# Dropping the zero columns behind the last K and Q heads and keeping one column of ones per chunk of three heads

## The chip, the cores and the metric

The kernel runs on one core of one Trainium2 chip. The core has a matrix engine (TensorE, PE in the profile; its weight loads are listed as PEld), a vector engine (VectorE, DVE), an activation engine (ScalarE, ACT), a general engine (GpSimd, POOL) and a queue that issues the DMAs (SyncE, SP). They run side by side and wait for each other through semaphores. The metric is the time of one execution on the device in microseconds (us); the time of a kernel is the median of its runs.

## The reference: what is computed

The input is 2048 tokens of 640 channels in bfloat16. They are normalized (layer norm without weights), and two branches are added to the input:

```python
xn  = layernorm(x)
out = x + A(xn) + B(xn)

# A: linear attention, H = 32 heads of Dh = 20 channels
q, k, v = split_heads(xn @ wqkv)
pq, pk  = q @ w_phi, k @ w_phi                       # per head, 20 x 20
phi_q   = concat(softmax(pq), softmax(-pq))          # 40 features per head
phi_k   = concat(softmax(pk), softmax(-pk))
kv      = phi_k^T v          # per head, summed over all tokens: 40 x 20
z       = sum of phi_k over the tokens               # 40
A       = ((phi_q kv) / (phi_q z + 1e-6)) @ wo

# B: gated linear unit with F = 1536
B       = (silu(xn @ w1) * (xn @ w3)) @ w2
```

## The kernel before, in words

Tokens are worked on in 16 tiles of 128 (`NST`), channels in 5 chunks of 128 (`KD`). Everything is written inside a manual schedule: each engine does its instructions in the order in which the code issues them, and the code interleaves the stages by hand.

The 32 heads are grouped in 11 chunks (`NCH`): ten of three heads and a last one of two (`HC`). A chunk takes 2 x 64 features: 60 of the positive softmax (three heads of 20), 4 of padding, and the same for the negative one, so that the features of one chunk fill 128 rows of the matrix engine. The last chunk has only 40 real features of each sign. The kernel keeps its shape by computing a 33rd head of zeros: the fused weights `wkphi` and `wqphi` have `FW` = 660 columns for 640 real ones, and the last 20 columns, filled with zeros by GpSimd in the first channel chunk (L190), are multiplied for that chunk alone (L300). Their exponentials are 1, so nothing special has to be done behind them. In a loop on the chip that runs only where the weights are too large for an exponential without its maximum taken off, the same helpers are used; it does not run here.

The stages, in order of time:

- *Start.* Inputs are loaded, layer norm statistics go through VectorE and GpSimd, xn is transposed (on TensorE and ScalarE for the first four tiles, by DMA for the others). `v_unit` (L311) computes V of a tile: ten matmuls of 320 columns in two PSUM banks, which ScalarE copies to `vaug` (L314) in two pieces. `vaug` holds, for each tile and each head, 20 channels of V and one 1, so that one matmul yields kv and z; the ones are filled once, by ScalarE for half the tiles (L196) and by GpSimd for the others (L200). GLU units (`glu_unit`, L398: ten matmuls of 512 columns; ScalarE takes a tanh, VectorE two products) are put between. Late in this stage `fuse` (L382) multiplies the key weights with `w_phi`; ScalarE copies the results to `wkphi` (L391), in turn with the copies of the last V units, in the order V(12), FB(0), FB(1), V(13), FB(2), V(14), FB(3), V(15), FB(4).
- *K rounds*, 16 of them. `phi_unit` multiplies a tile by `wkphi` (ten matmuls, L301, 360 columns in one bank and 280 or 300 in the other), ScalarE takes four exponentials (`exps`, L328: two signs for each of two banks), VectorE sums them by head (L361) and takes reciprocals (L363), GpSimd scales (L364). Two rounds later `kv_unit` (L424) multiplies phi, as weights, by the chunk's rows of `vaug` (63 columns, 42 for the last chunk) and adds up in a pair of PSUM banks kept through all rounds. GLU units fill the round; in five rounds `fuse` makes the query weights.
- *Q rounds*, 20 of them. The same for queries; in the second one `kv_done` (L437) copies the sums of `kv_unit` to `kvr`, leaving out with a mask (`own`) the products of one head's features with another's channels: three products on VectorE. phi is transposed by a DMA (L444), `r_unit` (L453) multiplies it by `kvr`, VectorE divides (L469 to L474), the result is transposed by a DMA (L499), and from the fifth round on `out_unit` (L516) multiplies by `w2` and `wo` and VectorE adds the input (L525).

Single PSUM banks come from one pool of six (`bank`), shared by V, fused weights, K, Q, GLU and output units; one double bank (`pair`) serves `kv_unit`, `r_unit` and every other `fuse`.

Of the kernel before, what the change touches and what calls it, by code (L numbers as in the profile page):

```python
# [8 lines left out]
P = 128  # L9
# [3 lines left out]
def kernel(  # L13
# [36 lines left out]
    NCH = 11  # L50
    HC = [3] * 10 + [2]
    CH = 6 * 3 * Dh

    FW = D + Dh

    PARTS = [
        (0, 0, 0, 7), (0, 1, 6, 13), (0, 2, 12, 16),
# [6 lines left out]
    one = ctx.enter_context(tc.tile_pool(name="one", bufs=1))  # L64
    work = ctx.enter_context(tc.tile_pool(name="work", bufs=2))
# [3 lines left out]
    def bank(name, dt=f32):  # L69
        n = 512 if dt == f32 else 1024  # L70
        return psum.tile([P, n], dt, name=name, tag="bank")

    def pair(name):
        return psum2.tile([P, 2, 512], f32, name=name, tag="pair")


    xnT = one.tile([P, KD, S], bf, name="xnT")
    wkphi = one.tile([P, KD, FW], bf, name="wkphi")
    wqphi = one.tile([P, KD, FW], bf, name="wqphi")
    w1 = one.tile([P, KD, F], bf, name="w1")  # L80
# [15 lines left out]
    wkT, wqT, wv = w_nat[:, 0], w_nat[:, 1], w_nat[:, 2]  # L96
# [1 line left out]
    phiqT = reg_w[:, KD * D : KD * D + 4 * NCH * P].rearrange(  # L98
        "p (n c s) -> p n c s", n=4, c=NCH
    )  # L100
    vaug = reg_v[:].rearrange("p (t h e) -> p t h e", t=NST, e=21)
    w2 = reg_v[:, 0 : KF * D].rearrange("p (c d) -> p c d", c=KF)
    oT = reg_v[:, KF * D : KF * D + KD * 512].rearrange("p (c s) -> p c s", c=KD)
    less = phi[:, 1].rearrange("p c g f -> p (c g f)")[:, 0 : 2 * FW].bitcast(f32)
# [14 lines left out]
    with tc.manual_schedule():  # L119
# [14 lines left out]
        def ld_wv(c, n):  # L134
# [21 lines left out]
            out=mask[:], in_=mask[:], pattern=[[8, KD], [-20, 8]], base=0,  # L156
# [3 lines left out]
            out=mask[:], in_=mask[:], pattern=[[-8, KD], [20, 8]], base=19,  # L160
# [4 lines left out]
        own = one.tile([P, 2, 3], bf, name="own")  # L165
        nc.gpsimd.memset(own[:], 1.0)
        nc.gpsimd.affine_select(
            out=own[:], in_=own[:], pattern=[[-64, 2], [-20, 3]], base=0,
# [3 lines left out]
            out=own[:], in_=own[:], pattern=[[64, 2], [20, 3]], base=19,  # L172
# [6 lines left out]
        nought = one.tile([P, P], bf, name="nought")  # L179
# [6 lines left out]
        warm(WARM)  # L186

        nc.gpsimd.memset(phi[:, :, :, :, 60:64], 0.0)
        for w in (wkphi, wqphi):
            nc.gpsimd.memset(w[:, 0, D:FW], 0.0)  # L190

        table = one.tile([P, 1], f32, name="table")
        nc.scalar.activation(out=table[:], in_=nought[:, 0:1], func=AF.Sqrt)
        nc.scalar.activation(  # L196
            out=vaug[:, 0:8, :, 20].rearrange("p t h -> p (t h)"),
            in_=nought[:, 0:1].to_broadcast([P, 8 * H]), func=AF.Identity, bias=1.0,
        )
        nc.gpsimd.memset(vaug[:, 8:NST, :, 20], 1.0)  # L200


        mv = one.tile([P, NST, 2], f32, name="mv")
# [85 lines left out]
        def tile_of(t):  # L289
            return slice(t * P, (t + 1) * P)  # L290

        def by_token(cols, w, name, cut, between=(KD, None)):


            ps = [bank(name), bank(name)]
            for c in range(KD):
                if c == between[0]:
                    between[1]()
                for i in range(2):
                    a, b = (0, cut) if i == 0 else (cut, w.shape[2] if c == 0 else D)  # L300
                    nc.tensor.matmul(  # L301
                        ps[i][:, 0 : b - a],
                        xnT[:, c, cols],
                        w[:, c, a:b],
                        start=(c == 0),
                        stop=(c == KD - 1),
                        skip_group_check=True,
                    )
            return ps

        def v_unit(t, cols=None, between=(KD, None)):  # L311
            ps = by_token(cols or tile_of(t), wv, "pv", HD, between)
            for i in range(2):
                nc.scalar.copy(  # L314
                    out=vaug[:, t, 16 * i : 16 * i + 16, 0:20],
                    in_=ps[i][:, 0:HD].rearrange("p (h d) -> p h d", d=Dh),
                )

        def halves(ps, dst):

            for i, n in ((0, 6), (1, 5)):
                c = slice(6 * i, 6 * i + n)
                yield ps[i][:, 0 : 60 * n], [dst[:, c, g, 0:60] for g in range(2)], n

        def exps(ps, dst):
            for p, to, n in halves(ps, dst):
                for g in range(2):
                    nc.scalar.activation(  # L328
                        out=to[g], in_=p.rearrange("p (c f) -> p c f", f=60),
                        func=AF.Exp, scale=1.0 - 2.0 * g,  # L330
                    )

        def exps_less_max(ps, dst):

            h0 = 0
            for p, _, n in halves(ps, dst):
                nc.scalar.copy(out=wide[:, Dh * h0 : Dh * (h0 + 3 * n)], in_=p)
                h0 += 3 * n
            w3 = wide[:, 0:FW].rearrange("p (h d) -> p h d", d=Dh)
            for g, op in ((0, ALU.max), (1, ALU.min)):  # L340
                top = work.tile([P, FW // Dh], f32, name="top")
                nc.vector.tensor_reduce(out=top[:], in_=w3, axis=AX.X, op=op)
                nc.gpsimd.tensor_tensor(
                    out=less[:].rearrange("p (h d) -> p h d", d=Dh), in0=w3,
                    in1=top[:, :, None].to_broadcast([P, FW // Dh, Dh]), op=ALU.subtract,
                )
                nc.scalar.activation(
                    out=dst[:, :, g, 0:60], in_=less[:].rearrange("p (c f) -> p c f", f=60),
                    func=AF.Exp, scale=1.0 - 2.0 * g,
                )  # L350

        def phi_unit(t, w, name, exps=exps, cols=None):

# [66 lines left out]
        def kv_unit(t, acc, first, last):  # L420

            for c in range(NCH):
                b, i = divmod(c, 6)
                nc.tensor.matmul(  # L424
                    acc[:, b, 63 * i : 63 * i + 21 * HC[c]],
                    phi[:, t % 4, c].rearrange("p g f -> p (g f)"),
                    vaug[:, t, 3 * c : 3 * c + HC[c], :],
                    start=(first and i == 0),
                    stop=last,
                    skip_group_check=True,  # L430
                )

        def kv_done(acc):

            for b, c0, n, k in ((0, 0, 6, 3), (1, 6, 4, 3), (1, 10, 1, 2)):
                a = 63 * (c0 - 6 * b)
                nc.vector.tensor_mul(  # L437
                    out=kvr[:, c0 : c0 + n, 0:k, :],
                    in0=acc[:, b, a : a + 21 * k * n].rearrange("p (c i e) -> p c i e", c=n, e=21),
                    in1=own[:, 0:1, 0:k, None].to_broadcast([P, n, k, 21]),  # L440
                )

        def phi_transposed(t):
# [250 lines left out]
        acc = pair("pkv")  # L694
# [51 lines left out]

    ok = nc.values_load(flag[0:1, 0:1], min_val=0, max_val=1)
    with tc.If(ok == 0):
        state = reg_v[:, 2048 : 2048 + 4 * 378].bitcast(f32).rearrange("p (b e) -> p b e", b=2)
        ld(wv, w_of(2))  # L750
        nc.gpsimd.memset(vaug[:, 0, :, 20], 1.0)
        nc.gpsimd.memset(state, 0.0)
        with tc.For_i(0, NST, 1) as t:
            cols = bass.ds(t * P, P)
            v_unit(0, cols)
            phi_unit(0, wkphi, "pk", exps_less_max, cols)
            acc = pair("pkv")
            kv_unit(0, acc, True, True)
            for i, n in ((0, 378), (1, 315 - 21)):
                nc.vector.tensor_tensor(  # L760
                    out=state[:, i, 0:n], in0=state[:, i, 0:n], in1=acc[:, i, 0:n], op=ALU.add
                )
        kv_done(state)
        ld(w2, B_w2.rearrange("(c p) d -> p c d", p=P))
        with tc.For_i(0, NST, 1) as t:
            rows = bass.ds(t * P, P)
            phi_unit(0, wqphi, "pq", exps_less_max, rows)
            phi_transposed(0)
            r_unit(0, quotient_by_pool)
            o_transposed(0)  # L770
            h = hT[:, bass.ds(t, 1)].rearrange("p a f s -> p (a f) s")
            res = out_unit(h, slice(0, P), residual(rows))
            ld(out2[rows, :], res[:])
# [28 lines left out]
```

## Time and profile before

| | |
|---|---|
| median of 3 runs | 271.1 us (270.97 to 271.72) |
| the profiled execution, its own time | 272.32 us |
| its span in the profile | 270.5 us |
| TensorE busy | 264.7 us, 98% of the span |
| VectorE, ScalarE, GpSimd busy | 188.5, 110.1 and 95.7 us |
| granted TensorE clock | full in all 40 slices |

The profile is of one execution; its rows are in microseconds from the start of the span. A group row names the line, the engine, the operation, the tiles written and read with their shapes, the count, then the busy time and the mean length of one in nanoseconds, and behind the next bar the idle time of the engine ahead of it and what ended it. A row of the chain has a start, a length, an engine and a line; the chain is followed back from the last instruction through whatever released each. A row of the timeline has a start, a length, an engine, an instruction and, in brackets, the idle time ahead.

### The profile page before, as it was taken

To read this page: it belongs to the slowest core of one execution; us is meant where nothing else is said; L and a number is where in the kernel's file an instruction comes from. 1 tells how busy PE (TensorE), PEld (TensorE's weight loads), DVE (VectorE), ACT (ScalarE), POOL (GpSimd) and SP (SyncE) were. 2 spreads that over 40 slices of the span, in tenths; PEclk is the share of its full clock that TensorE was granted. 3 is DMA by queue.
4 is the path that set the end of the run, shared out by engine and by line. 5 is a ranking of instruction groups with operands and counts; after the bars stand their busy time and mean duration, and the time that the engine had idled before them with its cause. 6 is when DMAs were issued, how large, how long until landed. Compare 5 with 4: busy or idle time off the path is not lost.

```text
span 270.5 us, 5193 instructions
## 1 busy us (share of the span) xinstructions
PE 264.7 (98%) x1990; PEld 166.6 (62%) x1990; DVE 188.5 (70%) x345; ACT 110.1 (41%) x263; POOL 95.7 (35%) x100
## 2 busy tenths in 40 slices
PE   8899999999999999999999999999999999999995
PEld 8546567555555555555555445677777777777773
DVE  4699950787777667777777788876766777776341
ACT  5653468543555554435655545422222222221000
POOL 5054740344443333333444321333344444433000
PEclk9999999999999999999999999999999999999999
DMA  6996547980000000000000864356676755675931
GB/s 200 339 242 121 68 87 181 299 197 28 0 0 2 0 2 0 0 5 0 0 2 0 221 179 84 82 121 137 117 151 137 142 129 126 130 148 129 152 98 55
DMA packets 63100, 27.80 MB, mean 103 GB/s; under 512 B 50144, under 2 KB 61792, under 8 KB 63072
## 3 DMA queue, kind: packets, MB, share of 16 engines
q1 hardware_dynamic: 63072, 27.43, 45.2%
q8 instruction: 17, 0.28, 0.4%
q14 instruction: 11, 0.09, 0.1%
HBM read 12.81 MB, written 2.62 MB: 57 GB/s over the span
## 4 chain that ended last, share of the span: by engine, by line
PE 89%; DVE 4%; DMA 2%; POOL 2%; issue 1%; SPq 1%; ACT 0%; DVEq 0%
PE acc L516 27%; PE gp L398 18%; PE up L398 18%; PE pq L301 8%; PE pk L301 8%; PE pv L301 5%; DMA reg_w<-in_A_wqkv_dram 2%; PE pkv L424 2%; PE pr L453 2%; DVE st L210 1%; PE pf L382 1%; SPq L109 1%; DVE reg_h L264 1%; POOL ry L224 1%; DVE gs L411 0%
## 5 line engine op out<-in xcount | busy, mean ns | idle before, releaser
L364 POOL TENSOR_TENSOR phi<-phi,rk 128x1320 bf16<-128x1320 bf16 x32 | 77.2, 2413 | 134.5 <-DVE rk L363 134.5
L361 DVE TENSOR_REDUCE sk<-phi 128x66 f32<-128x1320 bf16 x32 | 48.9, 1528 | 41.4 <-ACT phi L328 40.4
L398 PEld LDWEIGHTS <-w 128*128 128x128 bf16 x480 | 45.6, 98 | 50.6
L301 PEld LDWEIGHTS <-xnT 128*128 128x128 bf16 x480 | 45.3, 97 | 23.3 <-issue 2.0
L398 PE MATMUL up<-xnT,w 128*128 128x512 bf16 x240 | 59.6, 379 | 0.0
L398 PE MATMUL gp<-xnT,w 128*128 128x512 bf16 x240 | 59.6, 378 | 0.0
L516 PE MATMUL acc<-reg_v,reg_h 128*128 128x320 bf16 (+2 forms) x384 | 54.9, 299 | 0.0
L328 ACT ACTIVATE phi<-pq 128x360 bf16<-128x360 f32 (+1 forms) x64 | 23.3, 450 | 59.2 <-POOL phi L364 53.8
L516 PEld LDWEIGHTS <-reg_h 128*128 128x128 bf16 x384 | 37.3, 98 | 14.4
L406 ACT ACTIVATE th<-gp 128x512 f32<-128x512 f32 x48 | 28.8, 600 | 34.0 <-PE gp L398 30.4
L414 DVE SCALAR_TENSOR_TENSOR reg_h<-gs,up 128x512 bf16<-128x512 bf16 x48 | 33.0, 688 | 4.9
L328 ACT ACTIVATE phi<-pk 128x360 bf16<-128x360 f32 (+1 forms) x64 | 23.3, 451 | 24.5 <-PE pk L301 15.5
L411 DVE SCALAR_TENSOR_TENSOR gs<-th,gp 128x512 bf16<-128x512 f32 x48 | 31.5, 657 | 0.3 <-ACT th L406 0.3
L525 DVE TENSOR_TENSOR res<-acc,xr 128x320 bf16<-128x320 f32 (+2 forms) x32 | 14.3, 487 | 21.5 <-PE acc L516 21.5
L301 PE MATMUL pv<-reg_w,xnT 128*128 128x320 bf16 x160 | 23.9, 299 | 1.4 <-DMA reg_w<-in_A_wqkv_dram 1.1
L301 PE MATMUL pk<-wkphi,xnT 128*128 128x360 bf16 (+2 forms) x160 | 24.7, 300 | 0.0
L301 PE MATMUL pq<-wqphi,xnT 128*128 128x360 bf16 (+2 forms) x160 | 24.6, 299 | 0.0
L516 PE MATMUL acc<-reg_w,reg_v 128*128 128x320 bf16 (+2 forms) x160 | 24.5, 299 | 0.0
L363 DVE RECIPROCAL rk<-sk 128x66 f32<-128x66 f32 x32 | 18.1, 567 | 3.2
L516 PEld LDWEIGHTS <-reg_v 128*128 128x128 bf16 x160 | 15.7, 98 | 6.1
L210 DVE BATCH_NORM_STATS2 st<-reg_h 128x6 f32<-128x320 bf16 x32 | 13.8, 470 | 3.9 <-DMA reg_h<-in_A_x_dram 3.9
L314 ACT CAST reg_v<-pv 128x320 bf16<-128x320 f32 x32 | 12.1, 433 | 8.3 <-PE pv L301 8.2
(67 smaller groups left out, 134.6 us busy)
## 6 DMA issues: line engine op xcount, KB each, us to landing
w<-in_B_w_dram SPq DMA_DIRECT2D x2, 1280.0 KB, 8.8
xr<-in_A_x_dram SPq DMA_DIRECT2D x16, 160.0 KB, 2.5
out_dram<-res SPq DMA_DIRECT2D x15, 160.0 KB, 1.8
reg_h<-in_A_x_dram SPq DMA_DIRECT2D x7, 320.0 KB, 5.5
reg_v<-in_B_w_dram SPq DMA_DIRECT2D x4, 480.0 KB, 5.2
w<-in_B_w_dram SPq DMA_DIRECT2D x4, 320.0 KB, 6.6
reg_w<-in_A_wqkv_dram SPq DMA_DIRECT2D x2, 320.0 KB, 5.4
reg_w<-in_A_wo_dram SPq DMA_DIRECT2D x1, 480.0 KB, 4.3
```

Source lines behind the costliest of these rows:

```text
L210: nc.vector.bn_stats(out=st[:, i, :], in_=xt[:, i * HD : (i + 1) * HD])
L301: nc.tensor.matmul(ps[i][:, 0 : b - a], xnT[:, c, cols], w[:, c, a:b], start=(c == 0), stop=(c == KD - 1), skip_group_check=True,)
L328: nc.scalar.activation(out=to[g], in_=p.rearrange("p (c f) -> p c f", f=60), func=AF.Exp, scale=1.0 - 2.0 * g,)
L361: nc.vector.reduce_sum(out=sk[:], in_=rows, axis=AX.X)
L363: nc.vector.reciprocal(out=rk[:], in_=sk[:])
L364: nc.gpsimd.tensor_mul(out=rows, in0=rows, in1=rk[:, :, :, None].to_broadcast([P, 2 * NCH, 3, Dh]))
L398: nc.tensor.matmul(ps[:], w[:, c, fi * P : (fi + 1) * P], xnT[:, c, sc * 512 : (sc + 1) * 512], start=(c == 0), stop=(c == KD - 1),)
L406: nc.scalar.activation(out=th[:], in_=gp[:], func=AF.Tanh, scale=0.5)
L411: nc.vector.scalar_tensor_tensor(out=gs[:], in0=th[:], scalar=1.0, in1=gp[:], op0=ALU.add, op1=ALU.mult)
L414: nc.vector.scalar_tensor_tensor(out=hT[:, 4 * sc : 4 * sc + 4, fi, :], in0=gs[:].rearrange("p (t s) -> p t s", t=4), scalar=0.5, in1=up[: ...
L516: nc.tensor.matmul(ps[:, 0 : b - a], rows[j][0], rows[j][1][:, a:b], start=(j == 0), stop=(j == len(rows) - 1),)
L525: nc.vector.tensor_tensor(out=res[:, a:b], in0=ps[:, 0 : b - a], in1=xr[:, a:b], op=ALU.add)
```

## The change

The zero columns go. `wkphi` and `wqphi` get 640 columns, their GpSimd fills go, and the second bank of a K or Q unit gets 280 columns in every channel chunk. The 20 features of each sign that the last chunk has too many are filled once with ones in all four phi buffers, by GpSimd; they are summed and scaled with the others as before.

`vaug` holds one column of ones for each chunk of three heads, at its head, in place of one for each head: a chunk's row has `VC` = 61 columns (41 for the last). `kv_unit` streams 61 and 41 columns; z is the same for all heads of a row, and `kv_done` spreads it with a broadcast, so that it has six products in place of three. `kvr` keeps its form, and nothing behind it changes. All ones in `vaug` are filled by GpSimd.

Since the last chunk now ends at 40 features, ScalarE works in three pieces (`chunks`, in place of `halves`): 6 chunks from the first bank, 4 from the second, and the last one by itself. That makes six exponentials of 360, 240 and 40 columns a unit in place of four, and three V copies in place of two; V units cut their columns at 360, as K and Q units do.

```diff
-    FW = D + Dh
+    VC = 1 + 3 * Dh
...
-    wkphi = one.tile([P, KD, FW], bf, name="wkphi")
-    wqphi = one.tile([P, KD, FW], bf, name="wqphi")
+    wkphi = one.tile([P, KD, D], bf, name="wkphi")
+    wqphi = one.tile([P, KD, D], bf, name="wqphi")
...
-    vaug = reg_v[:].rearrange("p (t h e) -> p t h e", t=NST, e=21)
+    vaug = reg_v[:, 0 : NST * NCH * VC].rearrange("p (t c e) -> p t c e", t=NST, e=VC)
...
         nc.gpsimd.memset(phi[:, :, :, :, 60:64], 0.0)
-        for w in (wkphi, wqphi):
-            nc.gpsimd.memset(w[:, 0, D:FW], 0.0)
+        nc.gpsimd.memset(phi[:, :, NCH - 1, :, 40:60], 1.0)
...
-        nc.scalar.activation(
-            out=vaug[:, 0:8, :, 20].rearrange("p t h -> p (t h)"),
-            in_=nought[:, 0:1].to_broadcast([P, 8 * H]), func=AF.Identity, bias=1.0,
-        )
-        nc.gpsimd.memset(vaug[:, 8:NST, :, 20], 1.0)
+        nc.gpsimd.memset(vaug[:, :, :, 0], 1.0)
...
-                    a, b = (0, cut) if i == 0 else (cut, w.shape[2] if c == 0 else D)
+                    a, b = (0, cut) if i == 0 else (cut, D)
...
-            ps = by_token(cols or tile_of(t), wv, "pv", HD, between)
-            for i in range(2):
+            ps = by_token(cols or tile_of(t), wv, "pv", CH, between)
+            for p, c0, n, k in chunks(ps):
                 nc.scalar.copy(
-                    out=vaug[:, t, 16 * i : 16 * i + 16, 0:20],
-                    in_=ps[i][:, 0:HD].rearrange("p (h d) -> p h d", d=Dh),
-                )
+                    out=vaug[:, t, c0 : c0 + n, 1 : 1 + k],
+                    in_=p.rearrange("p (c e) -> p c e", c=n),
+                )
+
+        def chunks(ps):
+            yield ps[0][:, 0:CH], 0, 6, 60
+            yield ps[1][:, 0 : 4 * 60], 6, 4, 60
+            yield ps[1][:, 4 * 60 : D - CH], 10, 1, 40
 
         def exps(ps, dst):
-            for p, to, n in halves(ps, dst):
+            for p, c0, n, k in chunks(ps):
                 for g in range(2):
                     nc.scalar.activation(
-                        out=to[g], in_=p.rearrange("p (c f) -> p c f", f=60),
+                        out=dst[:, c0 : c0 + n, g, 0:k],
+                        in_=p.rearrange("p (c f) -> p c f", c=n),
                         func=AF.Exp, scale=1.0 - 2.0 * g,
                     )
...
-                    acc[:, b, 63 * i : 63 * i + 21 * HC[c]],
+                    acc[:, b, VC * i : VC * i + 1 + Dh * HC[c]],
                     phi[:, t % 4, c].rearrange("p g f -> p (g f)"),
-                    vaug[:, t, 3 * c : 3 * c + HC[c], :],
+                    vaug[:, t, c, 0 : 1 + Dh * HC[c]],
...
             for b, c0, n, k in ((0, 0, 6, 3), (1, 6, 4, 3), (1, 10, 1, 2)):
-                a = 63 * (c0 - 6 * b)
+                a, e = VC * (c0 - 6 * b), 1 + Dh * k
+                rows = acc[:, b, a : a + e * n].rearrange("p (c e) -> p c e", c=n)
                 nc.vector.tensor_mul(
-                    out=kvr[:, c0 : c0 + n, 0:k, :],
-                    in0=acc[:, b, a : a + 21 * k * n].rearrange("p (c i e) -> p c i e", c=n, e=21),
-                    in1=own[:, 0:1, 0:k, None].to_broadcast([P, n, k, 21]),
+                    out=kvr[:, c0 : c0 + n, 0:k, 0:20],
+                    in0=rows[:, :, 1:e].rearrange("p c (i d) -> p c i d", d=Dh),
+                    in1=own[:, 0:1, 0:k, None].to_broadcast([P, n, k, Dh]),
+                )
+                nc.vector.tensor_mul(
+                    out=kvr[:, c0 : c0 + n, 0:k, 20],
+                    in0=rows[:, :, 0:1].to_broadcast([P, n, k]),
+                    in1=own[:, 0:1, 0:k].to_broadcast([P, n, k]),
                 )
```

The helper of the loop that does not run (`exps_less_max`) is changed in the same manner.

More of the change, by code (lines that the diff above doesn't have):

```diff
@@ L100 @@
     )
-    vaug = reg_v[:].rearrange("p (t h e) -> p t h e", t=NST, e=21)
+    vaug = reg_v[:, 0 : NST * NCH * VC].rearrange("p (t c e) -> p t c e", t=NST, e=VC)
     w2 = reg_v[:, 0 : KF * D].rearrange("p (c d) -> p c d", c=KF)
     oT = reg_v[:, KF * D : KF * D + KD * 512].rearrange("p (c s) -> p c s", c=KD)
-    less = phi[:, 1].rearrange("p c g f -> p (c g f)")[:, 0 : 2 * FW].bitcast(f32)
+    less = phi[:, 1].rearrange("p c g f -> p (c g f)")[:, 0 : 2 * D].bitcast(f32)
     wide = one.tile([P, H * 21], f32, name="wide")
@@ L333, in exps_less_max @@
         def exps_less_max(ps, dst):
[L335 to L339, printed above, removed]
+            for p, c0, n, k in chunks(ps):
+                nc.scalar.copy(out=wide[:, 60 * c0 : 60 * c0 + k * n], in_=p)
+            w3 = wide[:, 0:D].rearrange("p (h d) -> p h d", d=Dh)
             for g, op in ((0, ALU.max), (1, ALU.min)):
-                top = work.tile([P, FW // Dh], f32, name="top")
+                top = work.tile([P, H], f32, name="top")
                 nc.vector.tensor_reduce(out=top[:], in_=w3, axis=AX.X, op=op)
@@ L344, in exps_less_max @@
                     out=less[:].rearrange("p (h d) -> p h d", d=Dh), in0=w3,
-                    in1=top[:, :, None].to_broadcast([P, FW // Dh, Dh]), op=ALU.subtract,
+                    in1=top[:, :, None].to_broadcast([P, H, Dh]), op=ALU.subtract,
                 )
-                nc.scalar.activation(
-                    out=dst[:, :, g, 0:60], in_=less[:].rearrange("p (c f) -> p c f", f=60),
-                    func=AF.Exp, scale=1.0 - 2.0 * g,
-                )
+                for c0, n, k in ((0, 10, 60), (10, 1, 40)):
+                    nc.scalar.activation(
+                        out=dst[:, c0 : c0 + n, g, 0:k],
+                        in_=less[:, 60 * c0 : 60 * c0 + k * n].rearrange("p (c f) -> p c f", c=n),
+                        func=AF.Exp, scale=1.0 - 2.0 * g,
+                    )
         def phi_unit(t, w, name, exps=exps, cols=None):
@@ L748 @@
     with tc.If(ok == 0):
-        state = reg_v[:, 2048 : 2048 + 4 * 378].bitcast(f32).rearrange("p (b e) -> p b e", b=2)
+        state = reg_v[:, 2048 : 2048 + 4 * 6 * VC].bitcast(f32).rearrange("p (b e) -> p b e", b=2)
         ld(wv, w_of(2))
-        nc.gpsimd.memset(vaug[:, 0, :, 20], 1.0)
+        nc.gpsimd.memset(vaug[:, 0, :, 0], 1.0)
         nc.gpsimd.memset(state, 0.0)
@@ L758 @@
             kv_unit(0, acc, True, True)
-            for i, n in ((0, 378), (1, 315 - 21)):
+            for i, n in ((0, 6 * VC), (1, 5 * VC - Dh)):
                 nc.vector.tensor_tensor(
```

4 lines of the change are left out of this document (removed).

## The prediction

> **What bounds the kernel now.** I read the page's busy shares and slices first, then the chain that ended last, then the groups by form, then the timeline of four stretches.
>
> ```profile
> PE 264.7 (98%) x1990; PEld 166.6 (62%) x1990; DVE 188.5 (70%) x345; ACT 110.1 (41%) x263; POOL 95.7 (35%) x100
> ...
> PE   8899999999999999999999999999999999999995
> ...
> PEclk9999999999999999999999999999999999999999
> ...
> PE 89%; DVE 4%; DMA 2%; POOL 2%; issue 1%; SPq 1%; ACT 0%; DVEq 0%
> ```
>
> TensorE is busy 98% of the span at the full granted clock, and the chain is 89% TensorE. So the first question of any edit is how much matmul time it takes out; the second is whether it makes TensorE wait somewhere. The 11% of the chain on other engines lies ahead of about 28 us, in the layer norm, and in the tail.
>
> ```profile
> 27.15 0.56 DVE gs L411
> ...
> 27.75 1.38 PE pv L301 x9
> ...
> 36.17 4.08 PE pv L301 x30
> ...
> 45.90 1.48 PE pk L301 x10
> ...
> 61.26 1.37 PE pk L301 x10
> ...
> 62.63 0.34 PE pkv L424 x11
> ...
> 203.67 1.38 PE pq L301 x10
> ```
>
> These rows of the chain (start, length, work) give prices by the unit: a V unit of ten matmuls takes 4.08 / 3 = 1.36 us, a K or Q unit 1.37 to 1.38 us, the eleven matmuls of `kv_unit` 0.34 us, and the first K unit, at 45.90, 0.1 us more than the others: it waits for something. From 27.75 us on nothing but TensorE work stands in the chain until the last unit, so that a wait put in there, or matmul time taken out, moves the end one for one.
>
> **The change part by part.** Rows by form first, since nearly every part changes a shape (mean ns of one behind the comma).
>
> ```profile
> L301 PE MATMUL pk<-wkphi,xnT 128*128 128x280 bf16 x64 | 17.6, 282 | 0.0
> ...
> L301 PE MATMUL pk<-wkphi,xnT 128*128 128x300 bf16 x16 | 4.7, 291 | 0.0
> ...
> L301 PE MATMUL pq<-wqphi,xnT 128*128 128x300 bf16 x16 | 4.6, 289 | 0.0
> ...
> L424 PE MATMUL pkv<-reg_v,phi 128*128 128x63 bf16 x160 | 7.6, 193 | 0.0
> ...
> L424 PE MATMUL pkv<-reg_v,phi 128*128 128x42 bf16 x16 | 2.9, 184 | 0.0
> ...
> L328 ACT ACTIVATE phi<-pk 128x360 bf16<-128x360 f32 x32 | 13.3, 468 | 24.5 <-PE pk L301 15.5 <-POOL phi L364 9.0
> ...
> L328 ACT ACTIVATE phi<-pk 128x300 bf16<-128x300 f32 x32 | 11.8, 433 | 0.0
> ...
> L195 ACT ACTIVATE table<-nought 128x1 f32<-128x1 bf16 x1 | 0.2, 202 | 0.0
> ...
> L196 ACT ACTIVATE reg_v<-nought 128x256 bf16<-128x256 bf16 x1 | 1.3, 1322 | 0.0
> ...
> L200 POOL MEMSET reg_v<- 128x256 bf16 x1 | 1.2, 1233 | 0.0
> ...
> L190 POOL MEMSET wkphi<- 128x20 bf16 x1 | 0.1, 115 | 0.0
> ...
> L437 DVE TENSOR_TENSOR kvr<-pkv,own 128x42 bf16<-128x42 f32 x1 | 0.2, 192 | 0.0
> ```
>
> *K and Q units.* The 20 columns of zeros go: the 32 matmuls of 300 columns become 280. By the means 290 - 282 = 8 ns each, 0.26 us in all. The chain offers a second price: a V unit streams the 3,200 columns that a K or Q unit will have, and takes 1.36 us against 1.375, so 15 ns a unit, 0.48 us in all; the excess over 8 ns would be the odd row length of 660 columns, which goes too. Ends 0.26 and 0.48; I take 0.40, nearer to the chain, which measures starts where the means are modelled ends.
>
> *kv_unit.* 63 columns become 61, and 42 become 41. Between the two forms lie 21 columns and 9 ns, 0.43 ns a column: 10 x 2 + 1 = 21 columns a unit, 9 ns, 16 units: 0.14 us. But a unit takes 0.34 / 11 = 31 ns a matmul, more than 63 x 0.43 = 27, so something other than columns has a part in it and may set all of it: the other end is nothing. I take 0.07. By the Trainium skill, *TensorE: Matmul & The Clock Gate*, "Wait — 56ns, not 53.3ns?", warm matmuls follow each other at N / 2.4 GHz plus about 2.5 ns and never under about 25 ns; that would make these 28.7 ns (the trace has 31), give 0.14 us here and 0.27 us for K and Q, an estimated sum of 0.41 us against my 0.47.
>
> *V units.* The cut moves from 320/320 to 360/280: the same 3,200 columns, so nothing on TensorE.
>
> *Exponentials and V copies in three pieces.* Here ScalarE gains instructions: 2 more for each of 32 phi units, 1 more for each of 16 V units. The stretch that matters is the one where it is fullest, V units between the fusing of the key weights:
>
> ```profile
> 43.81 0.76 ACT L314 CAST reg_v<-pv 128x320 bf16<-128x320 f32 x2 [0.26 <-PE pv L301]
> ...
> 44.45 0.77 ACT L391 CAST wkphi<-pf 128x320 bf16<-128x320 f32 x2
> ...
> 45.48 0.76 ACT L314 CAST reg_v<-pv 128x320 bf16<-128x320 f32 x2 [0.26 <-PE pv L301]
> ...
> 46.12 0.77 ACT L391 CAST wkphi<-pf 128x320 bf16<-128x320 f32 x2
> ...
> 47.30 1.46 ACT L328 ACTIVATE phi<-pk 128x360 bf16<-128x360 f32 x4 [0.40 <-PE pk L301]
> ```
>
> Two casts follow each other in 44.45 - 43.81 = 0.64 us, 0.32 each, where one lasts 0.43 (0.76 - 0.32): instructions overlap by 0.11. The trace has no piece of 40 columns. Low end: the one-column ACTIVATE, 0.202 - 0.11 = 0.09 us; high end: a whole 300-column one without overlap, 0.43. I take 0.13, near the low end, since 40 columns lie nearer to 1 than to 300. The other pieces change by the slope of the forms, 35 ns for 60 columns: a V unit's copies take 0.13 - 0.02 = 0.11 us longer, four exponentials turned into six 2 x (0.13 - 0.035) = 0.19 us.
>
> The V copies: ScalarE has 45.48 - 43.81 = 1.67 us a round and fills 4 x 0.32 = 1.28, so 0.11 more a round fits. But the last round ends in the casts at 46.12 to 46.89 of the last fused weights, for which the last matmuls of the first K unit wait: this is its extra 0.1 us. V(15)'s third piece pushes these casts back, and all behind them: +0.11 us on the path (ends 0.07 and 0.41). By the Trainium skill, *ScalarE: Activation LUTs*, "What ACT_TABLE_LOAD costs", an ACTIVATE costs a fixed part beside its columns and neighbours overlap by about 93 ns, which leaves an extra piece about 93 ns of its own, the elements being no more; by that estimate the delay is 0.09 us, and the overlap agrees with the 0.11 of the trace.
>
> The exponentials: sums (VectorE) and the scaling (POOL) start 0.19 us later each round. Who waits?
>
> ```profile
> 81.33 1.46 ACT L328 ACTIVATE phi<-pk 128x360 bf16<-128x360 f32 x4 [1.79 <-POOL phi L364]
> ...
> 82.82 1.53 DVE L361 TENSOR_REDUCE sk<-phi 128x66 f32<-128x1320 bf16 x1 [1.42 <-ACT phi L328]
> ...
> 201.81 0.57 DVE L363 RECIPROCAL rk<-sk 128x66 f32<-128x66 f32 x1
> ...
> 203.24 0.89 DVE L525 TENSOR_TENSOR res<-acc,xr 128x320 bf16<-128x320 f32 x2 [0.86 <-PE acc L516]
> ...
> 204.94 1.40 SPq L444 DMA_TRANSPOSE reg_w<-phi  x1
> ```
>
> In the K rounds VectorE stands idle 1.42 us ahead of the sums, and since each round shifts alike nothing piles up. In the Q rounds what lies behind the reciprocal is the result of `out_unit`, for which VectorE waits 0.86 us anyway; 0.19 goes into that. SyncE's queue holds, behind the transpose of phi, that of o_ and the load of xr; phi is wanted two rounds of 6.33 us later. So 0 on the path; cover gone above 0.86 us (four fifths of a piece without overlap: 2 x 0.40 = 0.80, just within).
>
> *Startup.* ScalarE loses the 1.32 us fill of ones (2.20 to 3.52 us, with the next work at 4.33): nothing waits for it. POOL loses two fills of 0.115 us and gains one of 160 ones, and fills 176 single ones in place of 256 (1.233 x 176 / 256 = 0.85 us): it ends no later. Zero, and if the fill took twice as long, the loads behind POOL's small casts would go out some 0.8 us late.
>
> *kv_done.* Three products become six. The three new ones have 18, 12 and 2 elements a row, the smallest row there is is 0.192 us for 42; so 3 x 0.11 to 3 x 0.19.
>
> ```profile
> 152.19 0.92 DVE L437 TENSOR_TENSOR kvr<-pkv,own 128x378 bf16<-128x378 f32 x3
> ...
> 153.03 0.68 DVE L411 SCALAR_TENSOR_TENSOR gs<-th,gp 128x512 bf16<-128x512 f32 x1
> ...
> 153.81 0.69 DVE L414 SCALAR_TENSOR_TENSOR reg_h<-gs,up 128x512 bf16<-128x512 bf16 x1
> ...
> 155.26 1.54 PE L301 MATMUL pq<-wqphi,xnT 128*128 128x360 bf16 x10
> ...
> 163.11 0.50 PE L453 MATMUL pr<-kvr,reg_w 128*128 128x63 bf16 x11
> ```
>
> kvr itself is wanted at 163.11. Queued behind kv_done are the products of three GLU units, whose banks TensorE takes again; the first ends at 154.50, and the Q unit that may take its banks starts at 155.26. Later by 0.19 + 0.33 (up to 0.57) it ends at 155.02 to 155.26: zero, but hardly more.
>
> **Sum.** -0.40 - 0.07 + 0.11 = -0.36 us of a span of 270.5. The profiled execution took 272.32, the median of the runs is 271.1; I take 0.36 from the median: 270.7 us. Ends: -0.62 + 0.07 = -0.55 and -0.26 + 0.41 = +0.15, so 270.5 to 271.3 for this case. What a measurement of this kernel can tell from no change is about 0.3%, 0.8 us; the forecast is within it.
>
> **Rivals.** *1. ScalarE becomes the bound from 40 to 47 us.* If a piece costs 0.43, each V unit adds 0.41, a round fills 1.69 of its 1.67 us; FB(0) and FB(1) stand without a V between them and leave a backlog near 0.36, to which V(15) adds 0.41: the casts come about 0.8 us late. -0.47 + 0.8 = +0.3: 271.4 us. For it: ScalarE is on the path there already. Against: every neighbouring pair of the trace overlaps. It decides from a piece of 0.4 us on.
>
> *2. The other side: banks.* All single banks come from one pool of six, and a unit may get one whose last reader is a product queued on VectorE behind layer norm work.
>
> ```profile
> 23.11 4.41 PE L301 MATMUL pv<-reg_w,xnT 128*128 128x320 bf16 x31
> ...
> 27.75 1.38 PE L301 MATMUL pv<-reg_w,xnT 128*128 128x320 bf16 x9 [0.24 <-DVE gs L411]
> ```
>
> It happens once: thirty matmuls of 0.136 us from 23.11 put the thirty-first at 27.2, the next should start at 27.36 and starts at 27.75, 0.39 us late. V units with a third copy give their second bank back later; if three or four more units between 23 and 45 us come to wait so, that is 1.2 to 1.6 us: 271.9 to 272.3, slower by 0.3%. From one such wait on (0.39 against 0.36) it is no longer faster. Against: on ScalarE the copies mostly wait for TensorE, with time to spare.
>
> *3. The same wait goes,* as the banks fall otherwise: -0.36 - 0.39 = -0.75; or the kv matmuls fall from 31 ns to what 61 columns need by columns alone, 61 x 0.43 = 26: 5 ns x 176 = 0.9, and the sum is -0.40 - 0.9 + 0.11 = -1.2, 269.9. The middle is 270.2.
>
> *4. The columns cost nothing,* because loading weights, not streaming, spaces these matmuls: -0 + 0.11: 271.2. Against: 360, 300 and 280 columns differ in the rows.
>
> **How the numbers follow.** Forecast 0.47 (within 0.3%); rival 1 0.08 and rival 4 0.05 (within); rival 2 0.16 (slower); rival 3 0.24 (faster by 0.3%). So faster 0.24, same 0.60, slower 0.16. The time is the forecast's, 270.7. Range: from rival 3 without its lower tail, 269.9, to rival 2's 272.0.
>
> **What would show it.** K and Q units at 1.36 us in the chain; kv units at 0.33 to 0.34; the first K unit at about 1.59 us in place of 1.48, with ScalarE's casts ahead of it ending near 47.0; six exponentials in 1.65 us; VectorE's idle time ahead of the result 0.67 in place of 0.86; no new wait of TensorE behind 28 us. It is wrong if TensorE's waits between 20 and 46 us change by more than 0.3 us, or if the pk and pq groups do not shrink by 0.3 us.

## The result and the profile after

| | before | changed |
|---|---|---|
| median of 22 runs each, us | 271.12 (270.81 to 271.79) | 270.71 (269.99 to 271.29) |
| ratio, with its 95% interval | 1 | 0.9978 (0.9970 to 0.9986) |
| the profiled execution, its own time, us | 272.32 | 270.34 |
| its span, us | 270.5 | 268.5 |

The kernel is 0.22% faster, 0.41 us by the medians: less than the 0.3% set as the bound of what one measurement tells, though 22 runs set it apart from no change. The forecast was 270.7.

First the page of the changed kernel: busy times, TensorE's slices, the chain by engine.

```profile
PE 263.7 (98%) x1990; PEld 166.2 (62%) x1990; DVE 188.7 (70%) x348; ACT 111.6 (42%) x342; POOL 95.3 (35%) x99
...
PE   8999999999999999999999999999999999999995
...
PE 89%; DVE 4%; POOL 2%; DMA 2%; issue 1%; SPq 1%; ACT 1%; DVEq 0%
```

TensorE has the same 1,990 matmuls and is busy 1.0 us less; ScalarE has 79 instructions more and 1.5 us more work, net of the fill of ones (1.32 us) that it lost; it now has 1% of the chain, where it had 0. Where, the chain shows (start, length, work):

```profile
3.18 4.56 DMA reg_w<-in_A_wqkv_dram
...
25.89 0.56 DVE gs L406
26.49 1.37 PE pv L295 x9
...
34.89 4.08 PE pv L295 x30
...
44.22 0.82 ACT reg_v L308 x3
45.04 0.67 ACT wkphi L386 x2
...
45.75 0.43 PE pk L295 x2
...
60.02 1.36 PE pk L295 x10
61.37 0.33 PE pkv L419 x11
...
208.29 1.36 PE pq L295 x10
```

Ten matmuls of a K or Q unit now take 1.36 us, as long as those of a V unit, and `kv_unit` 0.33. V(15)'s three copies and the two casts of the last fused weights stand in the chain ahead of the last two matmuls of the first K unit. The wait of V(7) for a product on VectorE (25.89, then 26.49) is as it was.

The span shrank by 2.0 us, five times as much as the medians. Most of that is one transfer of the start, which the change does not touch: the third load of the V weights lands 4.56 us after its issue here; in the profile of before it was

```profile
3.18 5.83 DMA reg_w<-in_A_wqkv_dram
```

and V(0) waits for it. So the two spans are not compared as wholes. From the fourth V unit on TensorE's work is fixed by the program, and starts of matmuls can be compared to some nanoseconds. The table gives, for all kernels of this study that bear on it, the time from the first matmul of a unit to the first one behind it (us; of the sixteen, the usual value), and two stretches: from V(3) to V(8), and from V(8) to the last matmul. V(n) is the V unit of tile n; the columns `kv` and `r` are `kv_unit` and `r_unit`, "first K" is the first K unit. Each row is of one profiled execution.

```
kernel             K unit  Q unit  kv     r      first K  V(7)   V(3) to V(8)  V(8) to last
before             1.374   1.370   0.342  0.342  1.482    1.755  18.03         235.73
changed            1.358   1.355   0.334  0.342  1.561    1.745  17.98         235.22
e1_zero_columns    1.358   1.355   0.342  0.342  1.482    1.755  18.03         235.28
e2_ones_column     1.374   1.370   0.333  0.342  1.563    1.750  17.99         235.68
e3_rows_660        1.363   1.359   0.333  0.342  1.562    1.743  17.98         235.35
e4_rows_64         1.358   1.355   0.312  0.320  1.562    1.758  18.02         234.51
e5_v15_by_vector   1.358   1.355   0.334  0.342  1.357    1.748  17.98         235.01
e8_g3_first        1.358   1.355   0.334  0.342  1.562    1.359  17.59         235.22
e10_together       1.358   1.355   0.312  0.320  1.357    1.359  17.61         234.30
```

By it the change is worth 0.51 us from V(8) on and 0.05 between V(3) and V(8): 0.56 us, inside the interval of the ratio (0.38 to 0.81 us). The groups by form of the changed kernel give the prices that the prediction had to bound (mean ns behind the comma):

```profile
L295 PE MATMUL pk<-wkphi,xnT 128*128 128x280 bf16 x80 | 21.9, 282 | 0.0
L322 ACT ACTIVATE phi<-pk 128x240 bf16<-128x240 f32 x32 | 10.2, 383 | 0.0
L322 ACT ACTIVATE phi<-pk 128x40 bf16<-128x40 f32 x32 | 5.3, 241 | 0.0
L308 ACT CAST reg_v<-pv 128x40 bf16<-128x40 f32 x16 | 3.5, 219 | 0.0
L419 PE MATMUL pkv<-reg_v,phi 128*128 128x61 bf16 x160 | 7.5, 192 | 0.0
L438 DVE TENSOR_TENSOR kvr<-pkv,own 128x18 bf16<-128x18 f32 x1 | 0.2, 224 | 0.0
L195 POOL MEMSET reg_v<- 128x176 bf16 x1 | 0.9, 887 | 0.0
```

And from the timeline (start, length, instruction, idle time ahead), the copies and casts before the first K unit, the six exponentials, and the two VectorE waits of a Q round:

```profile
44.22 0.82 ACT L308 CAST reg_v<-pv 128x360 bf16<-128x360 f32 x3 [0.20 <-PE pv L295]
44.91 0.79 ACT L386 CAST wkphi<-pf 128x320 bf16<-128x320 f32 x2
46.09 1.55 ACT L322 ACTIVATE phi<-pk 128x360 bf16<-128x360 f32 x6 [0.40 <-PE pk L295]
...
198.58 1.53 DVE L356 TENSOR_REDUCE sk<-phi 128x66 f32<-128x1320 bf16 x1 [0.98 <-ACT phi L322]
...
201.55 0.89 DVE L526 TENSOR_TENSOR res<-acc,xr 128x320 bf16<-128x320 f32 x2 [0.77 <-PE acc L517]
```

Three copies take 44.91 - 44.22 = 0.69 us to the next start, where two took 0.64; six exponentials take 1.55 us where four took 1.46. The idle time ahead of the result fell from 0.86 to 0.77 us, by just those 0.09.

### The profile page after: what moved, and what is told of

Same layout as the page of the kernel before. It is cut to its first block, busy times and chain, and to the rows that moved or that the text cites. A ratio compares the mean times of both kernels' runs of the same rounds, so it can differ in the third digit from the quotient of the medians.

```text
span 268.5 us, 5276 instructions
## 1 busy us (share of the span) xinstructions
PE 263.7 (98%) x1990; PEld 166.2 (62%) x1990; DVE 188.7 (70%) x348; ACT 111.6 (42%) x342; POOL 95.3 (35%) x99
## 4 chain that ended last, share of the span: by engine, by line
PE 89%; DVE 4%; POOL 2%; DMA 2%; issue 1%; SPq 1%; ACT 1%; DVEq 0%
PE acc L517 28%; PE gp L393 18%; PE up L393 18%; PE pq L295 8%; PE pk L295 8%; PE pv L295 5%; PE pr L454 2%; PE pkv L419 2%; DMA reg_w<-in_A_wqkv_dram 2%; DVE st L205 1%; PE pf L377 1%; SPq L109 1%; DVE reg_h L259 1%; POOL ry L219 1%; DVE gs L406 0%
## 5 line engine op out<-in xcount | busy, mean ns | idle before, releaser
L322 ACT ACTIVATE phi<-pq 128x360 bf16<-128x360 f32 (+2 forms) x96 | 24.8, 364 | 58.0 <-issue 44.1
L322 ACT ACTIVATE phi<-pk 128x360 bf16<-128x360 f32 (+2 forms) x96 | 24.8, 364 | 24.1 <-PE pk L295 24.1
L295 PE MATMUL pk<-wkphi,xnT 128*128 128x360 bf16 (+1 forms) x160 | 24.5, 299 | 0.0
L295 PE MATMUL pq<-wqphi,xnT 128*128 128x360 bf16 (+1 forms) x160 | 24.3, 299 | 0.0
L295 PE MATMUL pv<-reg_w,xnT 128*128 128x360 bf16 (+1 forms) x160 | 23.7, 299 | 0.4 <-DVE gs L406 0.2
L308 ACT CAST reg_v<-pv 128x360 bf16<-128x360 f32 (+2 forms) x48 | 13.2, 353 | 7.7 <-PE pv L295 7.6
```

The source lines that it names most:

```text
L295: nc.tensor.matmul(ps[i][:, 0 : b - a], xnT[:, c, cols], w[:, c, a:b], start=(c == 0), stop=(c == KD - 1), skip_group_check=True,)
L322: nc.scalar.activation(out=dst[:, c0 : c0 + n, g, 0:k], in_=p.rearrange("p (c f) -> p c f", c=n), func=AF.Exp, scale=1.0 - 2.0 * g,)
```

## The experiments

The theory: two gains of matmul time (K and Q units; kv units), one delay (V(15)'s third piece ahead of the first K unit), and covers that hold everywhere else. Rivals are named with each run. Medians are beside runs of the kernel before on the same chip.

**Each half by itself.** `e1_zero_columns` takes only the zero columns out; V copies and the ones stay as before:

```diff
 # before
-    wkphi = one.tile([P, KD, FW], bf, name="wkphi")      # wqphi likewise
+    wkphi = one.tile([P, KD, D], bf, name="wkphi")
...
-        for w in (wkphi, wqphi):
-            nc.gpsimd.memset(w[:, 0, D:FW], 0.0)
+        nc.gpsimd.memset(phi[:, :, NCH - 1, :, 40:60], 1.0)
...
-            for p, to, n in halves(ps, dst):
+            for p, c0, n, k in chunks(ps):
```

> The kernel before with the zero columns alone taken out: rows of 640 in wkphi and wqphi, six exponentials; V copies and the columns of ones as before. My theory: K and Q units fall from 1.373 to 1.358 us (20 columns fewer and a row length that suits the reads), 32 x 0.0145 = 0.46 us; the extra exponentials are covered, and the first K unit waits no longer than before (0.115 us), since the V copies stay at two. From V(8) on 0.46 us shorter, ratio to before about 0.9983. Rival, ScalarE's extra pieces are not free: six exponentials put something off that TensorE waits for, and the stretch from V(8) on shrinks by less than 0.3 us.

270.69 us, ratio 0.9979 (0.9970 to 0.9988). In the chain, the first K unit and a later one:

```profile
44.94 1.48 PE pk L299 x10
...
60.27 1.36 PE pk L299 x10
```

The first K unit waits as before (1.48 in place of 1.37 then), the others take 1.36. From V(8) on it is 0.45 us shorter, where 0.46 was expected. So the six exponentials cost nothing, and the rival falls.

`e2_ones_column` is the other half: one column of ones a chunk and three V copies, with zero columns and four exponentials kept.

```diff
 # changed kernel
-    wkphi = one.tile([P, KD, D], bf, name="wkphi")       # wqphi likewise
+    wkphi = one.tile([P, KD, FW], bf, name="wkphi")
...
-                    a, b = (0, cut) if i == 0 else (cut, D)
+                    a, b = (0, cut) if i == 0 else (cut, w.shape[2] if c == 0 else D)
...
-            for p, c0, n, k in chunks(ps):               # in exps
+            for p, to, n in halves(ps, dst):
```

> The kernel before with one column of ones a chunk alone, and V copies in three pieces; zero columns and four exponentials stay. My theory: kv units fall from 0.342 to 0.334 us, 16 x 0.008 = 0.13 us; the first K unit's wait grows by 0.08 to 0.1 us, since the third piece of V(15) pushes the last casts back; so 0.03 to 0.05 us gained from V(8) on, ratio 0.9998, nothing that can be told from 1. Rival: the delay of the first K unit comes from the six exponentials or from the 640 columns, not from the copies; then it stays at 0.115 us here and the gain is 0.13.

271.18 us, ratio 0.9997 (0.9988 to 1.0006).

```profile
44.95 1.10 PE pk L297 x8
46.05 0.03 issue
46.08 0.43 PE pk L297 x2
...
60.38 1.37 PE pk L297 x10
61.75 0.33 PE pkv L426 x11
```

kv units are at 0.333, and the first K unit is broken ahead of its last two matmuls: 1.56 us in all against 1.37. Gain and delay nearly cancel, 0.05 us from V(8) on. The delay comes with the V copies in three pieces, then, not with the exponentials or the 640 columns. The two halves add up: 0.45 + 0.05 against 0.51 together.

**Columns or rows.** `e3_rows_660` puts the 640 columns back into rows of 660:

```diff
-    wkphi = one.tile([P, KD, D], bf, name="wkphi")
-    wqphi = one.tile([P, KD, D], bf, name="wqphi")
+    wkphi = one.tile([P, KD, D + Dh], bf, name="wkphi")[:, :, 0:D]
+    wqphi = one.tile([P, KD, D + Dh], bf, name="wqphi")[:, :, 0:D]
```

> The changed kernel with wkphi and wqphi laid out in rows of 660 of which 640 are used, so that only where the rows begin goes back to before. My theory: the second half of the gain per K and Q unit is the row length, so a unit comes to 1.364 to 1.366 us (1.358 in the changed kernel, 1.373 before), 0.2 to 0.25 us in all. Rival: only columns count; the unit stays at 1.358.

270.75 us, ratio 0.9983 (0.9973 to 0.9993). The K unit comes to 1.363 us, between the two and a little under the 1.364 to 1.366 expected; in all K and Q units together lose 0.14 us, where 0.20 to 0.25 were expected. Of the 15 ns that a unit gained, 4 to 5 belong to where the rows begin and 10 to the columns; the count of columns explains 8 of these (20 x 0.42, from 282 ns at 280 columns and 316 at 360), and some 2 ns stay unexplained.

The kv units raise the same question: within one, the ten matmuls of 63 columns of the kernel before are 28 ns apart where a row of `vaug` begins at a multiple of 32 bytes or halfway between (counted from the start of `vaug`), and 31 to 35 elsewhere. `e4_rows_64` gives each row 64 elements in `vaug` and in `kvr`:

```diff
+    VS = 64
-    kvr = one.tile([P, NCH, 3, 21], bf, name="kvr")
+    kvr = one.tile([P, NCH, VS], bf, name="kvr")[:, :, 0:63].rearrange(
+        "p c (i e) -> p c i e", e=21
+    )
-    reg_v = one.tile([P, NST * H * 21], bf, name="reg_v")
+    reg_v = one.tile([P, NST * NCH * VS], bf, name="reg_v")
-    vaug = reg_v[:, 0 : NST * NCH * VC].rearrange("p (t c e) -> p t c e", t=NST, e=VC)
+    vaug = reg_v[:].rearrange("p (t c e) -> p t c e", t=NST, e=VS)
```

> The changed kernel with the rows of vaug (61 used) and of kvr (63 used) laid out in 64 elements, 128 bytes, so that every row begins at a multiple of 32 bytes; nothing else differs. My theory: matmuls of kv and r are 31 ns apart where the first of a bank are 28 since their rows begin at odd places; all should come to about 28 ns: kv units 0.334 to 0.308, r units 0.342 to 0.315 us, 16 x 0.053 = 0.85 us less than the changed kernel, ratio to before about 0.9947. Rival: loading the weights of 128 x 128 spaces them at 31 ns, whatever the rows: no change against the changed kernel, 0.9978.

269.90 us, ratio 0.9958 (0.9943 to 0.9972). From its chain:

```profile
61.57 0.30 PE pkv L422 x11
...
207.66 0.31 PE pr L457 x11
```

kv units fall to 0.312, r units to 0.320: 28 and 29 ns a matmul. 16 x (0.022 + 0.022) = 0.70 us, and V(8) to the last matmul is 0.71 us shorter than in the changed kernel (0.85 expected). Weight loads were the same, so they did not set the 31 ns. By the stretches, this layout gains more on top of the changed kernel (0.71 us) than the change under study did (0.56); it was not run on the kernel before.

**The wait of the first K unit.** In `e5_v15_by_vector` VectorE, idle then, makes V(15)'s copies:

```diff
-                nc.scalar.copy(
+                copy = nc.vector.tensor_copy if t == NST - 1 else nc.scalar.copy
+                copy(
```

> The changed kernel with the three copies of V(15) made by VectorE, which is idle then; ScalarE goes from the casts of FB(3) to those of FB(4). My theory: the first K unit waits for ScalarE's casts, which V(15)'s copies push back; they come some 0.5 to 0.7 us sooner and the unit falls from 1.561 to 1.358 us, 0.2 us less in all. Rival: what it waits for is the product of FB(4) itself or a weight load; then it stays near 1.56.

270.53 us, ratio 0.9972 (0.9959 to 0.9984). No ScalarE is left in the chain there:

```profile
44.87 1.36 PE pk L295 x10
```

0.20 us less from V(8) on: the added 0.08 and the 0.12 that the kernel before had too. `e6_v15_more_pieces` goes the other way, with the 40-column copy of V(15) made five times:

```diff
+                for _ in range(5 if t == NST - 1 and k == 40 else 1):
                     nc.scalar.copy(
```

> The changed kernel with the 40-column copy of V(15) made five times instead of once. My theory: four more pieces of 0.085 us put the casts of FB(4) back by 0.34 us, and the first K unit grows by as much, 1.56 to 1.90 us; all behind it moves by that. Rival: the third piece has no part in the wait; the unit stays at 1.56.

271.52 us, ratio 1.0004 (0.9994 to 1.0013); the first K unit takes 2.45 us.

```profile
44.64 0.82 ACT reg_v L309 x3
45.47 0.02 issue
45.49 0.20 ACT reg_v L309
...
46.16 0.19 ACT reg_v L309
46.35 0.67 ACT wkphi L387 x2
...
47.06 0.43 PE pk L295 x2
```

The four more copies take 0.89 us, and the unit is longer by 0.89: one for one, as expected. But one takes 0.22, not 0.085: each starts only where the one ahead of it has ended. In the trace each of these copies waits for a semaphore that the copy ahead of it sets, since both write the same place; no such wait stands between the three pieces in the changed kernel. So the program holds them apart, and the run does not show whether the engine by itself would overlap them. The size expected was wrong, the path was right.

**The cover of the exponentials.** `e7_q_more_pieces` repeats the last exponential sixteen times in every Q round:

```diff
             exps(ps, dst)
+            for _ in range(16 if name == "pq" and exps is plain else 0):
+                nc.scalar.activation(
+                    out=dst[:, 10:11, 1, 0:40],
+                    in_=ps[1][:, 240:280].rearrange("p (c f) -> p c f", c=1),
+                    func=AF.Exp, scale=-1.0,
+                )
```

> The changed kernel with sixteen more exponentials of 40 columns (the last one repeated) in each of the 16 Q rounds: 1.36 us more a round, beyond the 0.77 us for which VectorE waits ahead of the output's addition. By the prediction's words the cover is gone above 0.86 us: the addition comes 0.6 us late a round, and if TensorE waits for it, 12 rounds make 7 us more. Rival: the addition is late but its banks are not wanted for another round of 6.3 us, so TensorE does not wait and the time stays at the changed kernel's.

283.85 us, ratio 1.0478 (1.0438 to 1.0517). The dose was 3.73 us a round, and not the 1.36 that was meant: the repeated exponentials wait for each other by a semaphore in the same way. V(8) to the last matmul is 12.4 us longer than in the changed kernel. Where it hurt is telling. A later round, then one of the first:

```profile
216.54 1.52 PE L525 MATMUL acc<-reg_w,reg_v 128*128 128x320 bf16 x10
...
218.76 1.53 DVE L364 TENSOR_REDUCE sk<-phi 128x66 f32<-128x1320 bf16 x1 [1.92 <-ACT phi L355]
220.88 0.82 DVE L534 TENSOR_TENSOR res<-acc,xr 128x320 bf16<-128x320 f32 x2
221.31 3.73 ACT L355 ACTIVATE phi<-pq 128x40 bf16<-128x40 f32 x16
222.86 1.52 PE L525 MATMUL acc<-reg_w,reg_v 128*128 128x320 bf16 x10
```

```profile
157.54 0.31 PE L295 MATMUL pq<-wqphi,xnT 128*128 128x360 bf16 x1 [1.69 <-DVE gs L414]
158.34 1.37 PE L295 MATMUL pq<-wqphi,xnT 128*128 128x280 bf16 x9 [0.48 <-DVE reg_h L417]
```

The rounds from 192 to 230 us still follow each other at 6.32 us (222.86 - 216.54): VectorE adds the result without idling, later than before, and TensorE does not wait. Ahead of them it does: in the second Q round for a bank that the repeated exponentials still read, in the third to fifth for the products of GLU units queued behind the late sums, and then 1.2 us for the late result of the first output unit. Behind 248 us it waits for two late transposes and a late quotient. So both the theory and its rival hold in part. `e9_q_six_pieces` (six repetitions in place of sixteen) is the dose that was meant, 1.38 us a round:

> The run with sixteen repeated exponentials again with six: a repeated piece took 0.233 us there, not 0.085, so that six make the 1.4 us that were meant. With 3.7 us a round TensorE did not wait in the rounds with output units, but did in the first Q rounds, where GLU products are queued on VectorE behind the sums. Now, 0.6 us beyond the 0.77 us of cover: if only a cover beyond the round's free time of VectorE counts (0.77 us ahead of the addition and 0.98 ahead of the sums), no TensorE wait anywhere and the changed kernel's time. Rival: the first Q rounds have less room than the later ones; waits of some tenths of a microsecond ahead of the second and third Q units, in all up to 1.5 us.

271.42 us, ratio 1.0008 (0.9998 to 1.0018), 0.30% above the changed kernel.

```profile
153.97 0.31 PE L295 MATMUL pq<-wqphi,xnT 128*128 128x360 bf16 x1
...
154.02 0.69 DVE L417 SCALAR_TENSOR_TENSOR reg_h<-gs,up 128x512 bf16<-128x512 bf16 x1
...
154.76 1.37 PE L295 MATMUL pq<-wqphi,xnT 128*128 128x280 bf16 x9 [0.48 <-DVE reg_h L417]
```

The rival came true, at one place: the one wait in the whole Q part is at the third Q unit, behind `kv_done`: its second bank is free when VectorE's second product ends at 154.71. Its unit takes 2.00 us in place of 1.36, and its first matmul came 0.2 us late: 0.84 us of V(8) to the last matmul, 236.06 against 235.22. For a shift of some 1.4 to 1.5 us this leaves about 0.6 us of slack in the changed kernel at that place, the thinnest cover of the exponentials that these runs show. The changed kernel's own timeline agrees:

```profile
152.51 0.69 DVE L409 SCALAR_TENSOR_TENSOR reg_h<-gs,up 128x512 bf16<-128x512 bf16 x1
...
153.67 1.52 PE L295 MATMUL pq<-wqphi,xnT 128*128 128x360 bf16 x10
```

The product ends at 153.20, and the unit takes the second bank with its second matmul, 0.15 us behind its first, at 153.82: 0.62 us of slack. In the kernel before it was 155.41 - 154.50 = 0.91 us; the change used up 0.29 of it.

**The bank wait of V(7).** `e8_g3_first` puts two lines of the schedule the other way round:

```diff
-        stats(10, 2)
         g3()
+        stats(10, 2)
```

> The changed kernel with the products of the fourth GLU unit (g3) ahead of the layer norm statistics of tiles 10 and 11 on VectorE; the wait of V(7) for a bank is the same in both kernels so far (1.755 before, 1.745 changed, 1.358 without it). My theory: that wait goes and V(8) starts 0.39 us sooner after V(3); the later statistics have time. Rival: the VectorE chain of the layer norm sets this stretch, and the time lost there comes back as a wait of a later unit for its transposed tile, so that V(8) to the last matmul grows by as much.

270.19 us, ratio 0.9964 (0.9950 to 0.9977). In its chain the V units now stand in one piece:

```profile
23.92 3.38 PE pv L295 x25
```

V(7) takes 1.359 us, V(3) to V(8) is 0.39 us shorter, and V(8) to the last matmul as long as ever. So such a wait costs what it lasts.

**All three together.** `e10_together` has the edits of `e4_rows_64`, `e5_v15_by_vector` and `e8_g3_first`.

> The changed kernel with rows of 64 elements in vaug and kvr, V(15) copied by VectorE, and g3's products ahead of the statistics. If the three gains found are independent: 0.71 + 0.21 + 0.39 = 1.3 us less than the changed kernel from V(3) on, median near 269.4 us, ratio to before about 0.993. Rival: one wait covers another, and less than 1.0 us of it arrives.

269.13 us, ratio 0.9917 (0.9904 to 0.9931): faster than both kernels, and 0.6% below the changed one.

```profile
44.27 1.36 PE pk L298 x10
...
60.81 0.30 PE pkv L423 x11
...
206.90 0.31 PE pr L458 x11
```

By the stretches 0.37 + 0.92 = 1.29 us less than the changed kernel, the 1.3 of the sum. By the ratios to the kernel before, 0.9917 and 0.9978, the two differ by more, some 1.65 us; 1.29 would be a ratio of 0.9931, the end of the interval. Where more would come from is open: in the profiled executions V(3) starts at the same time, 11.90 us here and 11.87 in the changed kernel.

## Why the prediction was right, and where it was not

It was right in its kind, and its mechanisms are those that the runs show; that the median came within 0.01 us of the forecast is in part luck, since the steps sum to -0.56 us and not to -0.36, and the runs of one kernel are spread over about 1 us. By its steps:

- *K and Q units, -0.40 of 0.26 to 0.48.* Measured 0.47 (15 usual K units shorter by 0.230 us in all, 16 Q units by 0.240): the upper end, the chain's price and not that of the means. Of the 15 ns a unit the prediction gave 8 to the columns and the other 7 to the row length of 660; `e3_rows_660` shows 10 to 11 and 4 to 5.
- *kv_unit, -0.07 of 0 to 0.14.* Measured 0.13, 16 x 0.008. That "something other than columns has a part in it" was right for the 31 ns; it is where the rows begin, and `e4_rows_64` shows it. The 8 ns that a unit gained are the columns': at starts on a multiple of 16 bytes its matmuls went from 28.4 to 27.8 ns, at all others from 32.1 to 30.9.
- *V copies, +0.11 of 0.07 to 0.41.* Measured 0.08 on the first K unit, at the place and by the path named; `e5_v15_by_vector` and `e6_v15_more_pieces` show it from both sides. The piece of 40 columns was mis-sized: 0.085 us from start to start, below the low end of 0.09 that the one-column ACTIVATE gave, in place of 0.13. By the figures of the Trainium skill, *ScalarE: Activation LUTs*, "What ACT_TABLE_LOAD costs" (for an ACTIVATE with immediate scale and bias 186 ns and 0.833 ns a column, neighbours overlapping by 93 ns), 40 columns would make an estimated 0.126 us; the trace has less, and decides. The three copies of V(15) take 0.05 us longer than the two did (0.11 foreseen). The other 0.03 was not foreseen: with the cut at 360 the last matmul of V(15)'s first bank has 40 columns more, and the first copy starts 0.016 us later against the K unit; and the two casts take 0.012 us longer, for a reason not looked for.
- *Exponentials, later by 0.19, nothing on the path.* They are later by 0.09, and nothing waits (`e1_zero_columns`). What failed here is the limit of the cover: "cover gone above 0.86 us". In most rounds with output units it is not gone at 3.7 us (`e7_q_more_pieces`, from 192 to 230 us). What limits it first is the third Q unit, behind `kv_done`, with 0.62 us (`e9_q_six_pieces`).
- *kv_done, nothing "but hardly more".* Nothing it was, and the place is the thinnest, as the step said; three more products took 0.2 us rather than 0.33 (VectorE from 150.70 to 151.73 against 152.19 to 153.03 before), and the product behind had 0.62 us to spare.
- *Startup, zero.* The fill of 176 ones took 0.887 us, 0.85 foreseen. Not foreseen: V(5)'s wait of 0.04 us went. Why is open: the kernel before and `e1_zero_columns` have it, `e2_ones_column` and the changed kernel do not, and `e4_rows_64` has 0.02.

The sum is -0.47 - 0.13 + 0.08 - 0.04 = -0.56 us against -0.36: two gains taken too low, one delay taken too high. The median moved by 0.41.

Of the rivals, the bound by ScalarE (1) falls with the price of a piece, and so does (4) with 0.47 us gained. The banks (2 and 3) neither worsened nor got better: V(7) waits as before. That this wait is worth 0.39 us, as worked out there, is shown by `e8_g3_first`; and the other half of (3), kv matmuls spaced by their columns alone, did not come with 61 columns: rows of 64 elements bring 28 ns, not the 26 worked out there.

## What to carry to other kernels

In a kernel whose chain is one engine's work, price an edit by start-to-start times in the chain, from a unit that already has the shape to come, rather than by the means of the forms: the V unit gave the K unit's new time to 2 ns. More, smaller pieces on another engine cost nothing where the next on the path does not wait for them, so look for the one place where it does (here the last weights ahead of the first unit that uses them). And where a narrow matmul reads rows packed without gaps, rows padded to 64 elements are worth a try: here they gained more than the columns taken out.

## What the runs showed of the hardware that was not expected

- Eleven matmuls of 63 or 61 columns take 0.342 or 0.334 us with rows packed at 63 or 61 elements and 0.320 or 0.312 with rows of 64; each of 32 K and Q units loses 4 to 5 ns with rows of 660 in place of 640 elements. In the kv units the fast starts are those on a multiple of 16 bytes from the start of `vaug`, in both kernels (28.4 ns against 32.1 before, 27.8 against 30.9 with 61 columns). In `e3_rows_660` two of the ten matmuls of a unit are slower, the 280-column ones of the second and fourth channel chunk (123.7 ns in place of 119), whose rows begin 8 bytes off such a multiple (counted from the start of the weights' tile); the 360-column ones that begin so too are not slower. So the rule of the kv units is not a general one.
- On ScalarE a piece of 40 columns starts 0.085 us ahead of the next one if no semaphore stands between them, though it lasts 0.21 to 0.25. Where the next one writes the same place and the program makes it wait by a semaphore, the step is 0.22 to 0.23.
